# Norm's factor on GpSimd with a power, and a search that compares key less base with a constant table

## The chip, the cores and the metric

The kernel runs on one core of a Trainium2 chip. The metric is the device time of one execution in microseconds. Names of the engines in the rows: PE is TensorE, PEld its weight loads, DVE is VectorE, ACT is ScalarE, POOL is GpSimd, SP issues plain DMAs.

## What is computed

Three blocks on 3072 tokens of 512 features:

```python
# 1: attention in chunks of 32, with 16 left, 8 right and 8 memory keys
a = np.exp(scores - max);  a = a / (a.sum(-1) + 1e-9);  x = a @ v_full
# 2: routing: (token, expert) pairs by falling logit, 8 experts, at most 384 tokens each
for idx in np.argsort(-(x @ w_gate).flatten()):
    tok, e = idx // E, idx % E
    if assigned[tok] >= 0 or counts[e] >= cap: continue
    assigned[tok] = e; counts[e] += 1
out[assigned == e] = np.maximum(x[assigned == e] @ w1[e], 0) @ w2[e]
# 3: on that result
h = out @ w_in;  solu = h * softmax(h)
ln = (solu - mu) / np.sqrt(var + 1e-6) * g_ln;  y = ln @ w_out
```

## The kernel before

*Attention* (to about 146 us) works on 128 tokens at a time and ends with the gate's logits L in SBUF. *Route* then fills one expert a round: each token goes by its best expert left, as a 32-bit key, and `search` finds the largest 16-bit number that 384 keys of some expert reach, four bits at a time, first in the keys' upper half and then in the lower. There are 8 steps (it 0 to 3, twice) for each of seven experts; the eighth takes what is left.

One step: ge compares 24 keys of each partition with 15 thresholds (thr, or the constant table jtab in step 0); matrix products r count them by expert. For the first two experts there are 24 products and a second one ("sat", "some"). For the other five (`few`) there are 3 products, then on DVE d (the products' diagonal), n (its sum), q (n spread for the next product), one product, cmax and mx, the number of thresholds reached. From mx come the next thr, with jb (table plus base, made while PE counts), and the new base, lines 605 to 664.

*Experts*, in the order in which they fill: gather 384 tokens, `g12` (products h and y with w1 and w2), `g3` (w_in) with `soft` (c and the sums), `g4` (w_out) and a scatter of the rows ob. All products use a split of each operand into a high and a low part: ACT copies w1h and w2h, POOL subtracts (w1l, w2l, 128x512 each, 16 an expert), DVE makes hl, ll, xl and yl. POOL's queue also issues the indirect DMAs: weights, tokens, and the scatters behind a small memset (spacer). `norm`, line 1044, makes the factor k of each token from the sums in ss and sq, with 18 DVE instructions (na, nv, ny, nz, k; an inverse root by a shift and three Newton steps): once for three tiles together (3 columns), for the last expert once for each tile. k is read by the ACT instruction that makes ob, at the end of `g4` one stage later.

The order is not written out: `Pace` keeps a rough clock of each engine (its cost of each instruction is in `cost`, line 308) and emits the steps of routing, soft, norm and weight splits between PE's products when their inputs should be there. Each engine then runs in that order, so a product r that comes before its DVE input is ready holds up PE. Stage r, in what follows, is the stretch with g12 of expert r: stage 0 from 196 to 270 us, 1 to 335, and from there each runs from the start of one g4 to the next, 2 to 404, 3 to 482, 4 to 562, 5 to 642, 6 to 720. In stage r DVE also carries the search for expert r + 1 and, from stage 1 on, the norm of expert r - 1; in stages 0 and 1 the chunks of w_out too (v, e, out_l).

Of the kernel before, what the change touches and what calls it, by code (L numbers as in the profile page):

```python
# [10 lines left out]
F32 = mybir.dt.float32  # L11
# [18 lines left out]
DFF = 1024  # L30
# [25 lines left out]
def warm(nc, p, ident, n):  # L56
    """Keeps the tensor engine busy while it waits, so that its clock is up when the data come."""
    for i in range(n):
        nc.tensor.transpose(p[:, i % 4], ident, ident)


def attention(nc, tc, q, kx, vx, wgx, ident, x_dram, L, consts, beside):
    """Chunked attention of all heads, 128 tokens at a time, x to DRAM and the gate's logits to L."""
# [182 lines left out]
class Pace:  # L246
    """Work emitted in small steps beside the main products, when what it reads is about to be there.

    Each engine executes in program order, so that an instruction emitted too early holds up all that follows
    on its engine. A rough model of the core says when: the clocks (us) are where each engine will be after  # L250
    what has been emitted, "now" is the tensor engine's. A job is a generator. It yields what its next step
    waits for: a tile, an engine (the end of its last instruction), a time, or ("spare", engine): that the
    engine has nothing else to do."""
# [10 lines left out]
    def tile(self, ap):  # L264
        """Start, writes and reads of a tile. It starts when the tile before it in its place is done with."""
        t = self.tiles.get(ap.name)
        if t is None:
            start = 0.0
            if ap.space != DRAM:
                ring = self.rings.setdefault(ap.tensor.tag, [])  # L270
                bufs = ap.tensor.tag_meta.bufs
                if len(ring) >= bufs:
                    old = self.tiles[ring[-bufs]]
                    start = max([old[0]] + [x[4] for x in old[1] + old[2]]) + SIGNAL
                ring.append(ap.name)
            t = self.tiles[ap.name] = (start, [], [])
        return t
# [10 lines left out]
    def when(self, ap, eng="pe", write=False):  # L288
        """When ap can be read (or written) by the engine."""
        start, writes, reads = self.tile(ap)  # L290
        p0, p1, f0, f1 = self.region(ap)
        for w in writes + reads if write else writes:
            if w[0] < p1 and p0 < w[1] and w[2] < f1 and f0 < w[3]:
                start = max(start, w[4] + (SIGNAL if w[5] != eng else 0.125 if eng != "pe" and not write else 0.0))
        return start
# [88 lines left out]
    def soon(self):  # L384
        """When work that goes before will be there, less what a step may take."""
        return min([1e9] + [j[0] for j in self.jobs if j[2] < 2 and j[0] > self.now]) - self.fit

    def ready(self, *aps):
        """Lets time pass until the tensor engine finds these written."""
        while max(self.when(x) for x in aps) > self.now:  # L390
            self.tick()


class Timed:
    """The engines of nc, each instruction charged to pace."""
# [22 lines left out]
class Fixed:  # L418
    """w_in, and w_out times the norm's gain, each as a float32r part and the rest as another.

    The host hands over the float64 as they are: sign, 11 bits of exponent and the high 20 of the mantissa,
    then the low 32. Read as a float32 and times 2^-112 the first word has the exponent in its place but for
    three bits (v, once shifted); the second times the power of two is what v lacks."""
# [20 lines left out]
    def all(self, m, beside, every, a, b, lead=0.0):  # L444
        """Starts a chunk every so many us."""
# [68 lines left out]
    def need(self, m, beside, chunks):  # L514
        """Waits for these chunks, ahead of other work."""
# [5 lines left out]
    def take(self, what, n):  # L521
        """A place for one tile more, once one of n is free."""
# [5 lines left out]
class Route:  # L528
    """Greedy assignment by logit with a cap per expert, one expert filled per round.

    Each token left goes by its best expert left. The largest logit is sought (as a 32-bit key, four bits
    at a time, the keys' upper half and then the lower) above which some expert has CAP such tokens:
    that expert takes them, and what is left is the same problem."""
# [53 lines left out]
    def take(self):  # L587
        """The bank, when no other count is in it."""
# [8 lines left out]
    def search(self, key, oh, zero, r, late):  # L597
        """The largest 16-bit number that CAP keys of some expert reach; flags of such experts go on.

        few: of eight token tiles at once the products, then their sum by expert and threshold to all partitions,  # L600
        for fewer passes of the tensor engine; otherwise the way with the shortest chain."""
# [3 lines left out]
        base, thr, few, mid = zero, self.jtab[:, 0], late > LATE, NT if r else NT // 2  # L605
        for it in range(4):
            ge = self.t("ge", [NT, 15], BF)
            for c in (0,) if r else (0, mid):
                V.tensor_tensor(ge[:, c:c + mid], key[:, c:c + mid, None].to_broadcast([128, mid, 15]),
                                thr[:, None, :].to_broadcast([128, mid, 15]), op=ALU.is_ge)  # L610
            if last:
                last()
            if it < 3:
                jb = self.t("jb", [15])
                V.tensor_scalar(jb, self.jtab[:, it + 1], base, None, op0=ALU.add)
            yield "dve"
            p = yield from self.take()
            if few:
                for c in range(0, NT, 8):
# [5 lines left out]
                                op=ALU.mult)  # L625
                self.held = False
                n = self.t("n", [E], F16)
                with nc.allow_low_precision(reason="whole numbers up to 384"):
                    V.tensor_reduce(n[0:120], d[0:120].rearrange("p c e -> p e c"), axis=AX.X, op=ALU.add)
                q = self.t("q", [15, E], F16)  # L630
                V.tensor_tensor(q[0:120], n[0:120, None, :].to_broadcast([120, 15, E]), self.diag[0:120], op=ALU.mult)
# [26 lines left out]
            if it < 3:  # L658
                thr = self.t("thr", [15])
                V.scalar_tensor_tensor(thr, mx.to_broadcast([128, 15]), float(16 ** (3 - it)), jb,  # L660
                                       op0=ALU.mult, op1=ALU.add)
            nb = self.w.tile([128, 1], F32, tag="base", name="base", bufs=2)
            V.scalar_tensor_tensor(nb, mx, float(16 ** (3 - it)), base, op0=ALU.mult, op1=ALU.add)
# [113 lines left out]
    def compact(self, r, s1, sl):  # L777
        """The tokens taken, s1, by their slots sl: slot t * 128 + p to idx[p, t]."""
# [42 lines left out]
class Experts:  # L821
    """MoE of the experts in the order in which they fill, and the second block on their tokens."""

    def __init__(self, ctx, nc, tc, x_dram, w1, w2, fixed, route, beside, ident, out):
# [20 lines left out]
        self.spacer = k.tile([1, 1], F32, name="spacer")  # L845
        self.idx, self.iw = route.idx, route.iw
# [39 lines left out]
    def fetch(self, r, weights=True):  # L886
        """The tokens and the first weights of an expert, once they are known."""
# [22 lines left out]
    def bank(self, spare=False):  # L910
        """The transposes' bank, once its last tile is read; or one that is spare at the start."""
# [88 lines left out]
    def soft(self, r, t, h):  # L1000
        """c = h * exp(h - max) less its mean over the features; the sums that norm() takes.

        By halves, the maximum of the first while the products of the second run."""
# [34 lines left out]
        if r == E - 1:  # L1038
            yield 2.5
# [4 lines left out]
    def norm(self, r, s):  # L1044
        """k = 1/(sum+1e-9) / sqrt(var+1e-6), the token's factor of its output."""
        nc = self.nc
        ss, sq, k = (x[:, s] for x in self.Kc[r])
        s0, s1 = ss[:, :, 0], ss[:, :, 1]
        a, v, y, z = (self.sm.tile([128, TT], F32, tag=n, name=n, bufs=3)[:, s] for n in ("na", "nv", "ny", "nz"))
        V = nc.vector  # L1050
        V.scalar_tensor_tensor(a, s0, 1e-9, s1, op0=ALU.add, op1=ALU.add)
        yield 0.0
        V.reciprocal(a, a)
        yield 0.0
        V.tensor_tensor(v, a, a, op=ALU.mult)
        yield 0.0
        V.scalar_tensor_tensor(v, sq, 1.0 / DFF, v, op0=ALU.mult, op1=ALU.mult)
        yield 0.0
        V.tensor_scalar(v, v, 1e-6, None, op0=ALU.add)
        yield 0.0  # L1060
        V.tensor_scalar(y.bitcast(I32), v.bitcast(I32), 1, None, op0=ALU.logical_shift_right)
        V.tensor_scalar(v, v, -0.5, None, op0=ALU.mult)
        yield 0.0
        V.tensor_scalar(y.bitcast(I32), y.bitcast(I32), -1, 0x5F3759DF, op0=ALU.mult, op1=ALU.add)
        for _ in range(3):
            yield 0.0
            V.tensor_tensor(z, y, y, op=ALU.mult)
            yield 0.0
            V.tensor_tensor(z, z, v, op=ALU.mult)
            yield 0.0  # L1070
            V.scalar_tensor_tensor(y, z, 1.5, y, op0=ALU.add, op1=ALU.mult)
        yield 0.0
        V.tensor_tensor(k, a, y, op=ALU.mult)
# [44 lines left out]
    def run(self, steps):  # L1118
        """steps: the routing, a piece at a time, beside the products."""
# [110 lines left out]
def host(q, k, v, mem_k, mem_v, moe_w_gate, moe_w1, moe_w2, moe2_w_in, moe2_w_out, moe2_g_ln):  # L1230
    """Layouts of the inputs, in the types that they come in."""
# [45 lines left out]
```

## Time and profile before

| | |
|---|---|
| median of 3 runs | 859.87 us (857.61 to 862.3) |
| span of the profiled execution | 854.8 us |
| PE busy | 739.8 us, 87% |
| DVE busy | 563.6 us, 66%, 1667 instructions |
| POOL busy | 355.7 us, 42%, 360 instructions |
| chain that ended last | PE 55%, DVE 28%, DMA 10% |

A single time of the profiled execution is not listed beside the runs; its span is the time from its first instruction to its last, 5.1 us less than the median. All rows have line 406, since one helper records each operation: they are told apart by the tiles' names. An instruction's time counts from when its engine took it up to its end, so a wait inside it, for a port say, is part of it; a wait for a semaphore stands in brackets as idle time.

### The profile page before, as it was taken

To read this page: it belongs to the slowest core of one execution; us is meant where nothing else is said; L and a number is where in the kernel's file an instruction comes from. 1 tells how busy PE (TensorE), PEld (TensorE's weight loads), DVE (VectorE), ACT (ScalarE), POOL (GpSimd) and SP (SyncE) were. 2 spreads that over 40 slices of the span, in tenths; PEclk is the share of its full clock that TensorE was granted. 3 is DMA by queue.
4 is the path that set the end of the run, shared out by engine and by line. 5 is a ranking of instruction groups with operands and counts; after the bars stand their busy time and mean duration, and the time that the engine had idled before them with its cause. 6 is when DMAs were issued, how large, how long until landed. Compare 5 with 4: busy or idle time off the path is not lost.

```text
span 854.8 us, 14882 instructions
## 1 busy us (share of the span) xinstructions
PE 739.8 (87%) x5729; PEld 631.0 (74%) x5729; DVE 563.6 (66%) x1667; ACT 346.3 (41%) x681; POOL 355.7 (42%) x360
## 2 busy tenths in 40 slices
PE   5676787368998889899998999899899989999994
PEld 4555565257786777688887888788788889899883
DVE  6446466967999998789179838864984673163071
ACT  1344454122346444433183236324532643274170
POOL 6123232375556432652464146425532653464100
PEclk7899799557999999999999999999999999999997
DMA  9999899252135101510340042014101411330000
GB/s 204 238 240 224 200 218 362 90 181 87 38 114 173 35 13 38 184 50 1 105 166 2 14 156 103 1 58 165 50 1 62 162 48 38 115 120 1 38 1 37
DMA packets 37894, 88.32 MB, mean 103 GB/s; under 512 B 3904, under 2 KB 16320, under 8 KB 37824
## 3 DMA queue, kind: packets, MB, share of 16 engines
q1 hardware_dynamic: 24768, 41.23, 19.0%
q0 software_dynamic: 13056, 46.14, 16.2%
q8 instruction: 45, 0.74, 0.4%
q14 instruction: 25, 0.20, 0.1%
HBM read 74.78 MB, written 12.58 MB: 102 GB/s over the span
## 4 chain that ended last, share of the span: by engine, by line
PE 55%; DVE 28%; DMA 10%; issue 3%; SPq 1%; POOL 0%; ACT 0%; POOLq 0%; DVEq 0%
PE h L406 22%; PE o L406 16%; PE y L406 9%; DMA vd<-in_vx_dram 8%; DVE e L406 4%; PE r L406 3%; DVE ge L406 2%; PE tp L406 2%; DVE nz L406 2%; DVE q L406 2%; DVE thr L406 1%; DVE cmax L406 1%; DVE ohl L406 1%; DMA raw<-in_win_dram 1%; DVE hl L406 1%
## 5 line engine op out<-in xcount | busy, mean ns | idle before, releaser
L406 POOL TENSOR_TENSOR w1l<-raw,w1h 128x512 fp32r<-128x512 f32 x64 | 85.8, 1341 | 106.4 <-ACT w1h L406 103.9
L406 POOL TENSOR_TENSOR w2l<-raw,w2h 128x512 fp32r<-128x512 f32 x64 | 83.8, 1310 | 63.0 <-ACT w2h L406 60.7
L406 PE MATMUL y<-hh,w2h 128*128 128x384 f32 x256 | 92.0, 359 | 0.2 <-DVE e L406 0.2
L406 PE MATMUL y<-hl,w2h 128*128 128x384 f32 x256 | 89.8, 351 | 1.2 <-DVE hl L406 1.2
L406 PE MATMUL y<-hh,w2l 128*128 128x384 f32 x256 | 88.5, 346 | 0.0
L406 DVE TENSOR_REDUCE nm<-h 128x1 f32<-128x512 f32 x48 | 33.0, 687 | 77.0 <-PE h L406 77.0
L406 POOL DMA_INDIRECT out_dram<-ob,idx x24 | 24.5, 1022 | 136.6 <-ACT ob L406 135.5
L406 PE MATMUL o<-out_h,lh 128*128 128x512 f32 x192 | 77.0, 401 | 0.0
L406 PE MATMUL h<-in_h,yh 128*128 128x512 f32 x192 | 77.0, 401 | 0.0
L406 PE MATMUL h<-in_l,yh 128*128 128x512 f32 x192 | 76.1, 396 | 0.0
L406 PE MATMUL h<-in_h,yl 128*128 128x512 f32 x192 | 75.9, 395 | 0.0
L406 PE MATMUL o<-out_l,lh 128*128 128x512 f32 x192 | 75.1, 391 | 0.0
L406 PE MATMUL o<-out_h,ll 128*128 128x512 f32 x192 | 75.0, 391 | 0.0
L406 ACT ACTIVATE hh<-h 128x384 fp32r<-128x384 f32 x64 | 31.4, 491 | 101.7 <-PE h L406 91.1
L406 POOL DMA_INDIRECT raw<-in_w_dram,iw x64 | 62.8, 982 | 23.1 <-issue 15.7
L406 ACT CAST w2h<-raw 128x512 fp32r<-128x512 f32 x64 | 39.4, 618 | 64.7 <-PE y L406 38.8
L406 PE MATMUL h<-xh,w1l 128*128 128x384 f32 x256 | 64.0, 363 | 0.0
L406 PE MATMUL h<-xh,w1h 128*128 128x384 f32 x256 | 60.1, 355 | 0.7 <-ACT xh L406 0.7
L406 PE MATMUL h<-xl,w1h 128*128 128x384 f32 x256 | 60.5, 354 | 0.0
L406 POOL TENSOR_TENSOR p<-p,rec 128x512 f32<-128x512 f32 x22 | 22.9, 1042 | 79.8 <-DVE rec L406 56.3
L406 DVE SCALAR_TENSOR_TENSOR hl<-h,hh 128x384 fp32r<-128x384 f32 x64 | 35.2, 550 | 27.9 <-ACT hh L406 27.9
L406 PEld LDWEIGHTS y<-hl,w2h 128*128 128x128 f32 x256 | 49.1, 192 | 1.7 <-DVE hl L406 1.5
(197 smaller groups left out, 1771.2 us busy)
## 6 DMA issues: line engine op xcount, KB each, us to landing
vd<-in_vx_dram SPq DMA_DIRECT2D x48, 256.0 KB, 10.0
x_dram<-xs SPq DMA_DIRECT2D x6, 1024.0 KB, 9.0
kd<-in_kx_dram SPq DMA_DIRECT2D x12, 464.0 KB, 10.3
qt<-in_q_dram SPq DMA_DIRECT2D x6, 768.0 KB, 13.9
raw<-in_win_dram SPq DMA_DIRECT2D x16, 256.0 KB, 9.7
raw<-in_wout_dram SPq DMA_DIRECT2D x16, 256.0 KB, 2.7
qt<-in_q_dram SPq DMA_DIRECT2D x6, 256.0 KB, 6.8
kd<-in_kx_dram SPq DMA_DIRECT2D x8, 144.0 KB, 6.3
```

Of the source, the lines that this page charges most:

```text
L406: return fn(*args, **kw)
```

## The change

`norm` becomes six POOL instructions in place of 18 on DVE; the last is a power with exponent -0.5 from a constant tile, which one memset on DVE fills. The last expert's delay of 2.5 us ahead of it goes. In `search`, ge compares key less base with the table row of its step, so that thr and jb go; base is made by another form of instruction; n is written into the bank of the counts (PSUM, f32) and q reads it there. The comments of the functions are emptied too, which shifts line numbers.

```diff
@@ search
-        base, thr, few, mid = zero, self.jtab[:, 0], late > LATE, NT if r else NT // 2
+        base, few, mid = zero, late > LATE, NT if r else NT // 2
-                V.tensor_tensor(ge[:, c:c + mid], key[:, c:c + mid, None].to_broadcast([128, mid, 15]),
-                                thr[:, None, :].to_broadcast([128, mid, 15]), op=ALU.is_ge)
+                V.scalar_tensor_tensor(ge[:, c:c + mid], key[:, c:c + mid, None].to_broadcast([128, mid, 15]), base,
+                                       self.jtab[:, it, None, :].to_broadcast([128, mid, 15]),
+                                       op0=ALU.subtract, op1=ALU.is_ge)
-            if it < 3:
-                jb = self.t("jb", [15])
-                V.tensor_scalar(jb, self.jtab[:, it + 1], base, None, op0=ALU.add)
+                n = p[0:120, 8 * E:9 * E]
+                V.tensor_reduce(n, d[0:120].rearrange("p c e -> p e c"), axis=AX.X, op=ALU.add)
+                q = self.t("q", [15, E], F16)
+                V.tensor_tensor(q[0:120], n[:, None, :].to_broadcast([120, 15, E]), self.diag[0:120], op=ALU.mult)
                 self.held = False
-                n = self.t("n", [E], F16)
-                with nc.allow_low_precision(reason="whole numbers up to 384"):
-                    V.tensor_reduce(n[0:120], d[0:120].rearrange("p c e -> p e c"), axis=AX.X, op=ALU.add)
-                q = self.t("q", [15, E], F16)
-                V.tensor_tensor(q[0:120], n[0:120, None, :].to_broadcast([120, 15, E]), self.diag[0:120], op=ALU.mult)
-            if it < 3:
-                thr = self.t("thr", [15])
-                V.scalar_tensor_tensor(thr, mx.to_broadcast([128, 15]), float(16 ** (3 - it)), jb,
-                                       op0=ALU.mult, op1=ALU.add)
-            V.scalar_tensor_tensor(nb, mx, float(16 ** (3 - it)), base, op0=ALU.mult, op1=ALU.add)
+            V.tensor_scalar(nb, mx, float(16 ** (3 - it)), base, op0=ALU.mult, op1=ALU.add)
@@ Experts.__init__
+        self.power = k.tile([128, TT], F32, name="power")
+        nc.vector.memset(self.power, -0.5)
@@ soft
         if r == E - 1:
-            yield 2.5
             yield from self.norm(r, slice(t, t + 1))
@@ norm (all 18 instructions of before go; a yield stands between each of these)
+        G.tensor_tensor(a, ss[:, :, 0], ss[:, :, 1], op=ALU.add)
+        G.tensor_scalar(a, a, 1e-9, float(np.sqrt(1e-6 * DFF)), op0=ALU.add, op1=ALU.mult)
+        G.tensor_tensor(v, a, a, op=ALU.mult)
+        G.tensor_tensor(v, v, sq, op=ALU.add)
+        G.tensor_scalar(v, v, 1.0 / DFF, None, op0=ALU.mult)
+        G.tensor_tensor(k, v, self.power[:, s], op=ALU.pow)
```

DVE before, in stage 3 (about 447 to 451 us): the end of a search's second step, its third ge, the start of the norm, and the third step's q.

```order
L406 TENSOR_REDUCE cmax_6551<-r_6548 128x15
L406 TENSOR_SCALAR cmax_6551,mx_6553<-cmax_6551 128x15
L406 SCALAR_TENSOR_TENSOR thr_6555<-mx_6553,jb_6484 128x15
L406 SCALAR_TENSOR_TENSOR base_6557<-mx_6553,base_6480 128x1
L406 TENSOR_TENSOR ge_6559<-ki_6418,thr_6555 128x360
L406 TENSOR_SCALAR jb_6561<-jtab_150,base_6557 128x15
L406 SCALAR_TENSOR_TENSOR na_6580<-s_6294 128x3
L406 RECIPROCAL na_6580<-na_6580 128x3
L406 SCALAR_TENSOR_TENSOR hl_6571<-h_6537,hh_6570 128x384
L406 TENSOR_TENSOR d_6595<-r_6587,own_157 120x64
L406 TENSOR_REDUCE n_6597<-d_6595 120x8
L406 TENSOR_TENSOR q_6599<-n_6597,diag_166 120x120
```

DVE in the changed kernel, the same place: the second step's cmax to the third step's q.

```order
L406 TENSOR_REDUCE cmax_6358<-r_6353 128x15
L406 TENSOR_SCALAR cmax_6358,mx_6360<-cmax_6358 128x15
L406 TENSOR_SCALAR base_6362<-mx_6360,base_6291 128x1
L406 SCALAR_TENSOR_TENSOR ge_6364<-ki_6234,base_6362,jtab_150 128x360
L406 SCALAR_TENSOR_TENSOR hl_6375<-h_6345,hh_6374 128x384
L406 TENSOR_TENSOR d_6397<-r_6389,own_157 120x64
L406 TENSOR_REDUCE r_6389<-d_6397 120x8
L406 TENSOR_TENSOR q_6400<-r_6389,diag_166 120x120
```

thr, jb and the two na are gone; base has moved from behind thr to where thr stood, and ge follows it.

POOL before, in the same stage (about 443 to 453 us): two loads of weights and the subtractions of the next expert.

```order
L406 DMA raw1_5574<-in_w1_dram,iw3_5073 128x1024
L406 DMA raw2_5576<-in_w2_dram,iw3_5073 128x1024
L406 TENSOR_TENSOR w1l_5589<-raw1_5351,w1h_5588 128x512
L406 TENSOR_TENSOR w2l_5620<-raw2_5353,w2h_5619 128x512
L406 TENSOR_TENSOR w1l_5666<-raw1_5355,w1h_5665 128x512
L406 TENSOR_TENSOR w2l_5720<-raw2_5353,w2h_5719 128x512
```

POOL in the changed kernel, the same place (na, nv and k are the norm's, power the constant).

```order
L406 DMA raw1_5429<-in_w1_dram,iw3_4935 128x1024
L406 DMA raw2_5431<-in_w2_dram,iw3_4935 128x1024
L406 TENSOR_TENSOR w1l_5444<-raw1_5213,w1h_5443 128x512
L406 TENSOR_TENSOR w2l_5474<-raw2_5215,w2h_5473 128x512
L406 TENSOR_TENSOR na_5510<-s_5236 128x3
L406 TENSOR_SCALAR na_5510<-na_5510 128x3
L406 TENSOR_TENSOR nv_5511<-na_5510 128x3
L406 TENSOR_TENSOR nv_5511<-nv_5511,q_5237 128x3
L406 TENSOR_SCALAR nv_5511<-nv_5511 128x3
L406 TENSOR_TENSOR k_5238<-nv_5511,power_2018 128x3
L406 TENSOR_TENSOR w1l_5514<-raw1_5217,w1h_5513 128x512
L406 TENSOR_TENSOR w2l_5557<-raw2_5215,w2h_5556 128x512
```

The six instructions of the norm stand between a w2l and a w1l; the order of the rest is as before.

## Rows read from the trace of the kernel before

**Rows 1.** Page, part 1: busy us of each engine (share of the span) xinstructions.

```profile
PE 739.8 (87%) x5729; PEld 631.0 (74%) x5729; DVE 563.6 (66%) x1667; ACT 346.3 (41%) x681; POOL 355.7 (42%) x360
```

**Rows 2.** Busy us by stage: stretch, length, engines' busy (x), PEclk, DMA share, GB/s.

```profile
146.00:180.00 34.00, 12.39 (x249) 11.19 (x250) 30.32 (x127) 4.71 (x13) 15.76 (x16) 0.54 0.47 156
196.00:270.00 74.00, 66.53 (x493) 56.53 (x493) 65.61 (x171) 32.22 (x67) 41.19 (x40) 0.91 0.33 107
270.00:335.40 65.40, 58.25 (x336) 50.10 (x337) 60.79 (x193) 30.57 (x64) 22.03 (x20) 0.97 0.08 25
335.40:403.70 68.30, 61.41 (x363) 54.03 (x362) 55.77 (x166) 27.82 (x52) 34.26 (x33) 0.98 0.26 85
403.70:482.15 78.45, 75.01 (x407) 64.72 (x406) 51.52 (x172) 32.68 (x63) 35.03 (x34) 1.00 0.23 75
641.78:720.40 78.62, 75.43 (x428) 67.06 (x427) 44.94 (x117) 33.23 (x65) 38.70 (x36) 0.98 0.26 82
```

**Rows 3.** Waits of PE, 403.7 to 482.15 us: us in total, times, longest.

```profile
PE r L406 <- DVE q L406: 2.3, 4, 1.0
PE r L406 <- DVE ge L406: 0.9, 2, 0.7
```

**Rows 4.** Timeline, PE, DVE and POOL by turns: start, us, engine, operation, [idle before <-releaser].

```profile
349.24 5.61 DVE L406 TENSOR_TENSOR nz<-ny 128x3 f32<-128x3 f32 x1
...
349.83 1.29 POOL L406 TENSOR_TENSOR w1l<-raw,w1h 128x512 fp32r<-128x512 f32 x1
...
357.06 0.51 PE L406 MATMUL r<-oh,ge 128*120 128x64 bf16 x3 [3.40 <-DVE ge L406]
```

**Rows 5.** Timeline of stage 3 around one q and one thr.

```profile
449.78 1.28 POOL L406 TENSOR_TENSOR w1l<-raw,w1h 128x512 fp32r<-128x512 f32 x1 [1.85 <-ACT w1h L406]
...
449.85 1.28 DVE L406 TENSOR_TENSOR q<-n,diag 120x120 f16<-120x120 f16 x1
...
451.19 0.23 PE L406 MATMUL r<-q,ones 120*128 120x120 f16 x1 [0.58 <-DVE q L406]
...
452.36 0.86 PE L406 MATMUL h<-xh,w1l 128*128 128x384 f32 x4
...
454.74 0.17 DVE L406 SCALAR_TENSOR_TENSOR thr<-mx,jb 128x15 f32<-128x15 f32 x1
...
454.95 0.53 DVE L406 TENSOR_TENSOR ge<-ki,thr 128x360 bf16<-128x360 uint16 x1
```

**Rows 6.** Instructions by tile, DVE: xcount, duration ns min/median/max, first and last start.

```profile
L406 DVE TENSOR_TENSOR nz<-ny x30: 152/161/5609, 285.3 to 836.2; 128x3 f32<-128x3 f32 x21, 128x1 f32<-128x1 f32 x9
...
L406 DVE SCALAR_TENSOR_TENSOR thr<-mx,jb x30: 173/388/1070, 274.6 to 632.1; 128x15 f32<-128x15 f32 x30
...
L406 DVE TENSOR_TENSOR q<-n,diag x40: 220/222/1784, 272.3 to 634.3; 120x120 f16<-120x120 f16 x40
...
L406 DVE TENSOR_SCALAR jb<-jtab,base x28: 222/226/1256, 150.9 to 629.3; 128x15 f32<-128x15 f32 x28
...
L406 DVE TENSOR_TENSOR ge<-ki,thr x24: 332/532/880, 149.7 to 614.5; 128x360 bf16<-128x360 uint16 x18, 128x180 bf16<-128x180 uint16 x6
...
L406 DVE TENSOR_TENSOR d<-r,own x40: 208/213/226, 271.7 to 633.8; 120x64 f16<-120x64 f32 x40
...
L406 DVE SCALAR_TENSOR_TENSOR v<-v,e x32: 374/416/1512, 59.5 to 318.3; 128x256 int32<-128x256 int32 x32
```

**Rows 7.** The same for POOL, one tile.

```profile
L406 POOL TENSOR_TENSOR v<-v,in_h x16: 722/731/1513, 63.2 to 192.2; 128x256 f32<-128x256 f32 x16
```

**Rows 8.** Timeline, POOL: a DMA issue that waited for POOL's own w1l.

```profile
681.85 0.97 POOL L406 DMA_INDIRECT raw<-in_w_dram,iw  x1 [0.16 <-POOL w1l L406]
```

**Rows 9.** Timeline of the end: the last k and its reader.

```profile
836.75 0.16 DVE L406 TENSOR_TENSOR k<-na,ny 128x1 f32<-128x1 f32 x1
...
842.86 0.69 ACT L406 ACTIVATE ob<-o,k 128x512 f32<-128x512 f32 x1 [4.80 <-PE o L406]
```

More of the change, by code (lines that the diff above doesn't have):

```diff
@@ L1044, in norm @@
     def norm(self, r, s):
-        nc = self.nc
+        G = self.nc.gpsimd
         ss, sq, k = (x[:, s] for x in self.Kc[r])
[L1048 to L1051, printed above, removed]
+        a, v = (self.sm.tile([128, TT], F32, tag=n, name=n, bufs=3)[:, s] for n in ("na", "nv"))
+        G.tensor_tensor(a, ss[:, :, 0], ss[:, :, 1], op=ALU.add)
         yield 0.0
-        V.reciprocal(a, a)
+        G.tensor_scalar(a, a, 1e-9, float(np.sqrt(1e-6 * DFF)), op0=ALU.add, op1=ALU.mult)
         yield 0.0
-        V.tensor_tensor(v, a, a, op=ALU.mult)
+        G.tensor_tensor(v, a, a, op=ALU.mult)
         yield 0.0
-        V.scalar_tensor_tensor(v, sq, 1.0 / DFF, v, op0=ALU.mult, op1=ALU.mult)
+        G.tensor_tensor(v, v, sq, op=ALU.add)
         yield 0.0
-        V.tensor_scalar(v, v, 1e-6, None, op0=ALU.add)
+        G.tensor_scalar(v, v, 1.0 / DFF, None, op0=ALU.mult)
         yield 0.0
[L1061 to L1073, printed above, removed]
+        G.tensor_tensor(k, v, self.power[:, s], op=ALU.pow)
         for t in range(s.start, s.stop):
```

## The prediction

> **What bounds the kernel now.** I read the page's first part, then the busy times by stage, then the waits of PE in a stage, and last the timeline of DVE and GpSimd (POOL in the rows) around those waits. The page puts PE at 87% and DVE at 66% of 854.8 us [rows 1]. The stages say where that share hides a bound [rows 2]. From 146 to 180 us PE works 12.4 of 34.0 us: the first expert is sought and DVE's chain is the bound. From 196 us on PE sets the pace and only its gaps can be won: 74.00 - 66.53 = 7.5 us in stage 0, 65.40 - 58.25 = 7.2 in stage 1, 68.30 - 61.41 = 6.9 in stage 2, and 3.4 in stage 3 (78.45 - 75.01). Two more stages are like stage 3, and stage 6 has 3.2. That makes 13.5 us in stages 3 to 6 and 35 us from 196 to 720 us. The gaps of stage 3 are waits of the counting products r for DVE: 2.3 us for q and 0.9 us for ge [rows 3]. After 720 us no count is left.
>
> Why DVE is late there is the reading on which the rest stands. In stage 2 one nz, on 3 columns, takes 5.61 us, while POOL goes through its subtractions one after another from 349.83 us on; PE then stands 3.40 us in front of the first r [rows 4]. In stage 3 a q takes 1.28 us, as long as the w1l that POOL started just before it, and PE stands 0.58 us [rows 5]. Over the whole run nz has 0.152 us at best and 5.609 at worst, q 0.220 and 1.784, thr 0.173 and 1.070; d, as wide as a half of q but with one of its two inputs in PSUM, has 0.208 and 0.226 in 40 cases [rows 6]. So a DVE instruction that reads two tensors in SBUF waits out a POOL instruction, and one with an input in PSUM does not.
>
> **The norm.** 18 DVE instructions go, for seven experts on 3 columns and three times on 1. At nz's median of 0.161 us [rows 6] one norm is 18 x 0.161 = 2.9 us of DVE, and its waits come on top. In stage 3 its parts stand between the counts (the first order block of the change). They go for good.
>
> On POOL six instructions come, in one piece between two subtractions. Nothing of so few columns that reads tensors is in the trace there, and no power. A subtraction of 512 columns takes 1.28 us [rows 5] and one of 256 at best 0.722 [rows 7]: 2.2 ns a column, which leaves 0.16 us for the instruction itself. Each of the six waits for the one before; where POOL waited for its own result the gap was 0.16 us [rows 8]. I take 0.33 us each, 2.0 us a norm. The bounds: 1.0 us with no gaps; 6 x (0.72 + 0.16) = 5.3 us if each costs as much as 256 columns, the nearest full row; for the power alone I know no better end. Behind them in the queue stand w1l, w2l and then the DMAs of the next weights. What hides them: POOL sat idle 1.85 us before w1l at 449.78 us, and PE takes a w1l at 452.36, 1.3 us after that one's end [rows 5]: 3.15 us of room, or about 2.2 when PE gets there 1 us sooner (its waits at q gone). So 2.0 us fits closely, and I charge 1 us in all for seven norms.
>
> On that six the Trainium skill (GPSIMD Engine Reference, section 2.1 Instruction dispatch) adds one warning: the first call of newly loaded code on these cores costs about 6 us, unseen in the profile. No run here shows it; an estimate from that figure is one late w1l, some 4 us once, and a time near 848 us.
>
> The last expert's norms are off the path: k is ready at 836.75 us and its reader ob starts at 842.86 [rows 9], 6 us later. POOL's order puts a scatter of 0.97 us inside the last norm; that still fits. No gain and no loss there.
>
> **The search.** 42 thr and 42 jb go (14 searches, 3 each). What this is worth on the chain is little: ge starts 0.21 us after thr (454.74 to 454.95 [rows 5]), and now it has to follow base in the same way, so the chain keeps its length. thr's wait for POOL does not vanish: its median in the trace is 0.388 us against 0.173 at best, and ge, which still reads key and table from SBUF, inherits those 0.2 us. The jb, 0.226 us each, stood behind ge while PE counted; they delayed hl and e only. ge itself changes its form. The nearest row of the new form with two SBUF inputs is v, 256 columns in 0.416 us; ge's 360 in 0.532 us lie on the same line (104 columns more for 0.116 us) [rows 6], so I charge nothing; the bound above is its worst case so far, 0.880.
>
> A sentence of the skill speaks against that: in the Vector Engine (DVE) Microarchitecture Reference, section 7, this form with two SBUF sources that are not bf16 runs at half rate. The row of v says otherwise, since 256 columns at half of DVE's rate would be some 0.53 us without any start-up. I follow the row and keep the rule as a rival.
>
> n is now written to PSUM, and q reads it there. n I leave at 0.27 us. q loses its fast form: by d's 0.213 us for 64 columns and 1.1 ns for each of 56 more it takes 0.27 us in place of 0.222, and it no longer waits for POOL. Over 40 cases that is +2 us of DVE against waits of up to 1.78 us. The ge waits remain.
>
> **The sum**, in PE's gaps. Stages 3 to 6: of 13.5 us I leave 1.25 a stage (the ge waits as they are, and a rest), so -8.5. Stage 2: the 3.40 us behind nz, and 0.6 of the rest, -4.0: m and ge of that search now run before POOL's series begins. Stage 1: DVE is 60.79 us busy in 65.4, and loses a norm (2.9 us and waits) and 8 x (0.23 + 0.17) = 3.2 us; I take half of the gap, -3.5. Stage 0: its search reads counts from PSUM and its thr never waited; -0.5. The first search, 146 to 180 us: the same chain, 0 (from -1, if ge meets POOL less often, to +1.5, if more often). POOL +1. Together -15.5 us: the profiled execution would go from 854.8 to 839.3. The median of the runs, 859.87, lies 5.1 us above that span, so 844.4 us. The ends: all gaps from 196 us on gone gives 825; every term nothing and POOL's upper bound gives more than before.
>
> **The rivals.**
> First, the waits move: ge takes what thr and q waited, and PE waits for ge. For it: 40 ge with two SBUF inputs stay in the same places beside the same subtractions. Against: q's four waits a stage are the larger half, and a q cannot wait any more. Price: 40 x 0.2 = 8 us back, time 852. By the skill (SBUF — State Buffer, Who interferes with whom) two SBUF inputs contend with a POOL instruction that reads SBUF; the new norm is 60 such instructions more, which points this way.
>
> Second, slower: the norm on POOL. From 3.15 us a norm on, w1l comes late and PE waits at h in each of seven stages. At the bound of 5.3 us it is 3.1 us with PE's gain (5.3 - 2.2), 7 x 3.1 = 22 us, against which the gains of 16.5 stand: 865. Between, at 0.5 us an instruction, 3.0 a norm, it costs 6 us and the time is 849. For it: nothing shows a power on POOL. Against: the room in [rows 5].
>
> Third, ge at half rate, by the rule above: 360 columns at 1.1 ns more each make 0.39 us on 40 ge, and half of that on each of the 16 steps of the first two experts, some 19 us of chain, perhaps half of it before PE: 854.
>
> Fourth, more than I take: DVE gets ahead in stages 0 and 1 too, and the granted clock, 0.91 of full in stage 0 [rows 2], rises with fewer gaps: 10 us more, 834.
>
> **How the numbers follow.** My forecast 0.62, the moved waits 0.17, POOL slower 0.09, ge at half rate 0.04, the larger gain 0.08. Below 836 and above 857 I leave about a tenth each, so 836 to 857. What can be told from no change here is 0.5%, 4.3 us. Faster by more: the forecast, the larger gain and two thirds of the moved waits, 0.82; same 0.09, slower 0.09.
>
> **What would show it.** PE's gaps in stages 3 to 6 at 1 to 1.5 us each; no r behind a q; the 3.40 us before the first r of stage 2 gone; q never above 0.35 us; ge's mean up from 0.53 to 0.7 or so; six POOL instructions in about 2 us, and no h that waits for w1l. I am wrong if PE waits for w1l after each norm, if ge takes 0.9 us with POOL idle, or if the gaps stay and only their releaser changes from q to ge.

## The result, and the profile after

The changed kernel is faster, by more than was forecast. The first comparison, of four runs of each kernel, gave a ratio of 0.9691 [0.9648, 0.9733] to the kernel before; a second, six runs against 29 of before, gave 0.9782 [0.9742, 0.9822]. On 859.87 us these are 833 and 841 us, against a forecast of 844.4 and a range from 836: the first lies below the range, the second in it, and only 3 us from the forecast.

The two differ mainly in the kernel before, with a median of 861.1 us in the first and 854.7 in the second (839.2 and 836.4 for the changed kernel); why it was slower in the first is not shown. Slow runs are left out of the ratios, of the changed kernel's first four and of psum_only's the profiled one (844.97 and 860.08 us). In the profiles a part that the change does not touch varies: from the start to the first count of the search, the attention, the 14 profiled executions of this study take between 140.0 and 157.6 us. So the executions are compared from the first count to the end, and by stages; the changed kernel's second execution (span 833.4 us, attention 149.4) is shown, as its attention is nearest to that of before (148.2).

The page's first part, changed kernel (answers to [rows 1]):

```profile
PE 734.6 (88%) x5729; PEld 628.8 (75%) x5729; DVE 502.9 (60%) x1404; ACT 344.1 (41%) x681; POOL 376.3 (45%) x420
```

Busy times by stretch, in the columns of [rows 2]. Stages 0 and 1 are cut here at the expert's first product h, the later ones where a g4 starts. First the kernel before: from the first count to the end, stages 0 to 2 one by one, stages 3 to 6 in one piece.

```profile
148.22:854.80 706.58, 635.24 (x3783) 550.70 (x3783) 480.56 (x1462) 283.66 (x559) 307.07 (x296) 0.95 0.23 75
187.72:264.53 76.81, 70.80 (x504) 60.80 (x504) 68.35 (x171) 34.13 (x72) 46.13 (x44) 0.88 0.33 106
264.53:335.20 70.67, 60.30 (x349) 51.83 (x347) 66.02 (x203) 31.82 (x65) 24.59 (x23) 0.98 0.10 32
335.20:402.59 67.39, 60.50 (x348) 53.41 (x347) 54.83 (x166) 27.18 (x51) 34.26 (x33) 0.97 0.26 86
402.59:720.17 317.58, 304.11 (x1708) 263.51 (x1708) 211.41 (x655) 132.43 (x258) 144.22 (x136) 0.99 0.23 76
```

The changed kernel: first count to end, first search, stages 0 to 6 one by one, stages 3 to 6 in one piece.

```profile
149.43:833.43 684.00, 627.97 (x3783) 546.74 (x3783) 420.15 (x1198) 281.70 (x559) 328.04 (x356) 0.95 0.23 76
149.43:189.54 40.11, 16.92 (x271) 14.58 (x272) 30.26 (x111) 6.11 (x15) 20.35 (x20) 0.54 0.40 119
189.54:266.98 77.44, 69.92 (x503) 59.46 (x504) 65.18 (x163) 33.28 (x73) 45.36 (x44) 0.89 0.34 107
266.98:332.22 65.24, 58.92 (x352) 51.16 (x351) 61.09 (x179) 32.02 (x67) 32.23 (x34) 1.00 0.15 44
332.22:396.29 64.07, 59.66 (x344) 53.06 (x343) 43.74 (x126) 26.16 (x50) 32.17 (x35) 0.97 0.23 79
396.29:471.56 75.27, 75.00 (x420) 65.42 (x420) 46.67 (x148) 33.09 (x65) 37.34 (x40) 1.00 0.23 78
471.56:547.47 75.91, 75.60 (x432) 65.66 (x432) 49.53 (x153) 32.99 (x65) 37.40 (x39) 1.00 0.24 77
547.47:623.49 76.02, 75.60 (x433) 65.66 (x433) 49.51 (x154) 33.02 (x65) 37.47 (x39) 1.00 0.23 77
623.49:698.75 75.26, 73.79 (x428) 65.32 (x427) 38.33 (x93) 33.08 (x66) 41.43 (x42) 1.00 0.26 86
396.29:698.75 302.46, 299.98 (x1709) 262.05 (x1708) 184.04 (x547) 132.18 (x258) 153.65 (x160) 1.00 0.24 79
```

From the first count to the end 706.6 us have become 684.0: 22.6 us less (the other execution has 687.2, 19.4 less). Of these, 317.58 - 302.46 = 15.1 us lie in stages 3 to 6, where PE's gaps (length less PE's busy time) fell from 13.5 to 2.5 us. In stages 3 to 5 they are 0.3 to 0.4 us each, and PE there waits for no q and no ge [rows 3].

DVE by tile (answers to [rows 6]: min/median/max in ns):

```profile
L406 DVE SCALAR_TENSOR_TENSOR ge<-ki,base,jtab x24: 393/689/3575, 151.0 to 596.6; 128x360 bf16<-128x360 uint16 x18, 128x180 bf16<-128x180 uint16 x6
L406 DVE SCALAR_TENSOR_TENSOR ge<-lo,base,jtab x24: 401/594/1582, 160.7 to 611.9; 128x360 bf16<-128x360 f32 x18, 128x180 bf16<-128x180 f32 x6
...
L406 DVE TENSOR_TENSOR q<-r,diag x40: 281/283/284, 273.6 to 613.6; 120x120 f16<-120x120 f32 x40
L406 DVE TENSOR_SCALAR base<-mx,base x30: 212/214/216, 280.1 to 615.3; 128x1 f32<-128x1 f32 x30
...
L406 DVE TENSOR_SCALAR lo<-ki,base x7: 229/629/1231, 158.3 to 600.5; 128x24 f32<-128x24 uint16 x7
```

ge still waits, as forecast. q never does, and neither does base, whose waits the prediction had not looked at; lo, which reads one tensor and base by a pointer, does. POOL's norm and a ge ahead of it, in the stage that [rows 5] shows of before:

```profile
440.00 1.29 POOL L406 TENSOR_TENSOR w2l<-raw,w2h 128x512 fp32r<-128x512 f32 x1
...
440.54 1.14 DVE L406 SCALAR_TENSOR_TENSOR ge<-ki,base,jtab 128x360 bf16<-128x360 uint16 x1
441.25 0.48 POOL L406 TENSOR_TENSOR na<-s 128x3 f32<-128x3 f32 x1
...
441.82 0.20 POOL L406 TENSOR_SCALAR na<-na 128x3 f32<-128x3 f32 x1
442.10 0.19 POOL L406 TENSOR_TENSOR nv<-na 128x3 f32<-128x3 f32 x1
442.37 0.20 POOL L406 TENSOR_TENSOR nv<-nv,q 128x3 f32<-128x3 f32 x1
442.65 0.24 POOL L406 TENSOR_SCALAR nv<-nv 128x3 f32<-128x3 f32 x1
442.98 0.90 POOL L406 TENSOR_TENSOR k<-nv,power 128x3 f32<-128x3 f32 x1
443.86 1.28 POOL L406 TENSOR_TENSOR w1l<-raw,w1h 128x512 fp32r<-128x512 f32 x1
```

The norm takes 443.86 - 441.25 = 2.6 us, and no h waits for a w1l. At the end, k is ready 3 us before its reader (6 before, [rows 9]), so the tail of both is the same:

```profile
812.34 0.57 POOL L406 TENSOR_TENSOR k<-nv,power 128x1 f32<-128x1 f32 x1
815.97 0.69 ACT L406 ACTIVATE ob<-o,k 128x512 f32<-128x512 f32 x1 [3.60 <-PE o L406]
```

### The profile page after: what moved, and what is told of

It is laid out like the page before. It is cut to its first block, busy times and chain, and to the rows that moved or that the text cites. A ratio compares the mean times of both kernels' runs of the same rounds, so it can differ in the third digit from the quotient of the medians.

```text
span 843.0 us, 14682 instructions
## 1 busy us (share of the span) xinstructions
PE 735.2 (87%) x5729; PEld 630.4 (75%) x5729; DVE 502.6 (60%) x1404; ACT 343.9 (41%) x681; POOL 375.7 (45%) x420
## 3 DMA queue, kind: packets, MB, share of 16 engines
q1 hardware_dynamic: 24768, 41.23, 19.3%
## 4 chain that ended last, share of the span: by engine, by line
PE 59%; DVE 21%; DMA 13%; issue 3%; ACT 2%; SPq 1%; POOL 1%; POOLq 0%; DVEq 0%; ACTq 0%
PE h L406 25%; PE o L406 15%; PE y L406 11%; DMA vd<-in_vx_dram 5%; DVE e L406 3%; DVE ge L406 3%; PE tp L406 3%; PE r L406 3%; DMA kd<-in_kx_dram 2%; DVE ohl L406 2%; DMA raw<-in_win_dram 2%; DMA qt<-in_q_dram 1%; DVE hl L406 1%; DMA xg<-x_dram,idx 1%; PE s L406 1%
## 5 line engine op out<-in xcount | busy, mean ns | idle before, releaser
L406 POOL TENSOR_TENSOR w2l<-raw,w2h 128x512 fp32r<-128x512 f32 x64 | 86.4, 1350 | 47.6 <-ACT w2h L406 46.4
L406 PE MATMUL h<-xh,w1l 128*128 128x384 f32 x256 | 61.1, 357 | 0.0
L406 PE MATMUL r<-oh,ge 128*15 128x8 bf16 (+1 forms) x504 | 25.8, 180 | 30.5 <-DVE ge L406 30.0
```

Of the source, the lines that this page charges most:

```text
L406: return fn(*args, **kw)
```

## The experiments

Theory A, the prediction's: a DVE instruction that reads two tensors in SBUF waits out a POOL instruction, and PE's gaps are those waits. Rival B: DVE is simply loaded, and any 3 us less would do. A third cause stood beside both: the order, that is which DVE instruction meets which subtraction.

All runs in one table, in us. "First count to end" leaves the attention out. "DVE's waits" are the mean of stages 3 to 5: for each DVE instruction its time less the shortest of the same tile and shape, summed where it is over 0.06 us. The last four columns stand on one execution of each kernel. The changed kernel's other execution has 687.2, 302.6, 2.5 and 2.4, so the stages repeat better than the third column; the ratios do not all follow that column either (norm_only is 4.8 us shorter than before in it, and 0.55% slower over twelve runs), and a few us in it show nothing.

| kernel | ratio to before | first count to end | stages 3-6 | PE's gaps there | DVE's waits a stage |
|---|---|---|---|---|---|
| before | | 706.6 | 317.6 | 13.5 | 8.3 |
| changed | 0.9782 [0.9742, 0.9822] | 684.0 | 302.5 | 2.5 | 2.4 |
| norm_only | 1.0055 [1.0028, 1.0082] | 701.8 | 317.2 | 14.3 | 8.8 |
| search_only | 0.9931 [0.9902, 0.9961] | 698.5 | 315.1 | 13.4 | 5.6 |
| psum_only | 0.9975 [0.9948, 1.0002] | 700.4 | 314.6 | 13.2 | 7.1 |
| ge_only | 1.0100 [1.0058, 1.0142] | 709.2 | 323.9 | 19.3 | 8.1 |
| dve_free18 | 0.9835 [0.9797, 0.9874] | 684.3 | 308.7 | 6.9 | 3.6 |
| dve_port18 | 1.0028 [0.9992, 1.0064] | 703.7 | 316.2 | 14.3 | 6.5 |
| after_oldbase | 0.9822 [0.9781, 0.9863] | 689.3 | 310.4 | 9.9 | 5.6 |
| before_halves | 0.9944 [0.9910, 0.9979] | 697.7 | 318.4 | 12.0 | 7.4 |
| before, norm 4 us later | 0.9910 [0.9879, 0.9941] | 696.5 | 310.2 | 9.2 | 6.7 |
| changed, norm 4 us later | 0.9729 [0.9655, 0.9803] | 680.7 | 302.7 | 3.4 | 2.6 |
| table_in_psum | 0.9694 [0.9648, 0.9740] | 674.2 | 300.8 | 2.1 | 1.5 |

**The changed kernel again.** No edit.

> The changed kernel once more, for a second profile and more runs. Theory A (PE's gaps in stages 3 to 6 are what it gains; in the first profile a stage there is 76.0 us long with 0.4 us of gaps, against 79.8 and 3.4 before): the four stages again come to some 302 us against 316.8, and from the first count of the search to the end the kernel takes 687 us against 706.6, so about 20 us are won after the attention and nothing in it (148 us of attention as before): ratio 0.975 to 0.979. Rival B (the change also shortens something ahead of the stages): the attention or the first search is shorter than the 148.2 and 39.5 us of before by 5 us or more, ratio 0.970 or less.

684.0 us from the first count and 302.5 in the four stages: theory A's numbers. Neither the attention (149.4) nor the first search (40.1) is shorter than before.

**The parts alone.** norm_only takes the new norm, search_only the new search, psum_only and ge_only the two halves of the search (code shortened here and below):

```
psum_only:  n = p[0:120, 8 * E:9 * E]            # n and q as in the change; thr, jb, base, norm as before
ge_only:    V.scalar_tensor_tensor(ge, key, base, jtab, op0=subtract, op1=is_ge)   # thr, jb gone, new base;
                                                                                    # n, q, norm as before
```

> Only the norm goes to GpSimd; the search is the one of before. Theory A (the gaps are waits of q, thr and nz behind GpSimd; the norm brings the 3.4 us of stage 2, the search brings stages 3 to 6): PE's gaps in stages 3 to 6 keep 2 us or more of their 3.4, since q and thr still read two tensors in SBUF; 5 to 8 us are won, ratio 0.991 to 0.994. Rival B (DVE's load: any 3 us less per stage would do, since DVE then is ahead of PE): the gaps of stages 3 to 6 fall below 1 us with the norm alone, 15 us or more are won, ratio 0.982 or less. Rival C (the norm costs on GpSimd): h waits for w1l, ratio 1.0 or more.

> Only the search changes (comparison of key less base, count in PSUM); the norm stays on DVE. Theory A: q no longer waits for GpSimd, thr and jb are gone; gaps of stages 3 to 6 fall from 3.4 to 1 us or so each, stage 2 keeps the 3.4 us behind nz; 8 to 12 us won, ratio 0.986 to 0.991. Rival B (DVE's load): 3 us less per stage as well (9 us of busy time over the run for jb and thr each some 15), so the gaps fall by about half, 6 us won, ratio 0.993. If norm alone and search alone add up to the whole (20 us), the parts act by themselves; if each alone brings most of it, what counts is that DVE is early enough once.

> Only n is written to PSUM and q reads it there; thr, jb, ge and the norm are as before. Theory A: the 2.3 us a stage that PE waits at q go in stages 3 to 6 (q at most 0.3 us), the 0.9 us at ge stay: gaps 1.2 us a stage, 9 us won, ratio 0.989. Rival B (DVE's load): q is 0.06 us longer and the load is no smaller, so the wait goes to the next instruction and the gaps stay at 3 us: ratio 1.000.

> Only the comparison of key less base (thr and jb gone, base by a scalar); n and q in SBUF, norm on DVE as before. Theory A: q and nz still wait, base and thr no longer: stalls of stages 3 to 5 from 8.3 to 6 us, gaps of stages 3 to 6 of 10 to 13 us, 313 to 317 us. Rival B (thr and jb, or base, are the gain by themselves): 306 us or less.

In stages 3 to 6 the norm alone brings 0.3 us, the search alone 2.5, both 15.1; the comparison alone costs 6. Theory A missed the ratio of all four, and the gaps of all but norm_only. Rival B had psum_only right (gaps of 3.3 us a stage, 0.9975) and the ratio of search_only (0.9931), where the gaps did not fall as it said. The third cause named for norm_only, a late w1l, had its ratio (1.0 or more), but no h waits for w1l there. Neither A nor B had a part that makes the kernel slower. PE's waits in the four stages (us in total, times, longest), kernel before:

```profile
PE r L406 <- DVE q L406: 6.9, 12, 1.0
PE r L406 <- DVE ohl L406: 2.9, 3, 1.7
PE r L406 <- DVE ge L406: 2.8, 6, 0.7
```

search_only:

```profile
PE r L406 <- DVE ge L406: 7.5, 6, 1.9
PE r L406 <- DVE ohl L406: 3.0, 3, 1.7
PE r L406 <- DVE c L406: 2.3, 3, 0.8
```

and psum_only:

```profile
PE r L406 <- DVE ge L406: 8.2, 9, 2.0
PE r L406 <- DVE ohl L406: 2.9, 3, 1.7
PE r L406 <- DVE q L406: 1.3, 3, 0.5
```

The waits for q went to ge: the prediction's first rival came true in both, and not in the whole. One place in search_only shows how:

```profile
437.18 1.29 POOL L406 TENSOR_TENSOR w2l<-raw,w2h 128x512 fp32r<-128x512 f32 x1 [0.81 <-ACT w2h L406]
437.29 1.20 DVE L406 TENSOR_SCALAR ny<-nv 128x3 int32<-128x3 int32 x1
...
439.47 0.27 DVE L406 TENSOR_REDUCE cmax<-r 128x15 f32<-128x120 f32 x1
...
439.82 1.26 POOL L406 TENSOR_TENSOR w1l<-raw,w1h 128x512 fp32r<-128x512 f32 x1 [1.35 <-ACT w1h L406]
...
440.24 1.23 DVE L406 SCALAR_TENSOR_TENSOR ge<-ki,base,jtab 128x360 bf16<-128x360 uint16 x1
441.53 0.35 PE L406 MATMUL r<-oh,ge 128*120 128x64 bf16 x3 [1.93 <-DVE ge L406]
```

The norm's ny, which reads one tensor only, waits out w2l, cmax comes 1 us late for that, and so ge meets the next subtraction. In norm_only base does the same; its shortest is 0.146 us:

```profile
L406 DVE SCALAR_TENSOR_TENSOR base<-mx,base x30: 146/154/1301, 287.0 to 640.1; 128x1 f32<-128x1 f32 x30
```

**Load or port.** The changed kernel with eighteen DVE instructions that do no work of the kernel in each norm of experts 0 to 6, of two kinds:

```
dve_free18:  V.tensor_scalar(dz, dz, 0.5, ss[:, 0, 0:1], op0=mult, op1=add)    # dz: 1 column
dve_port18:  V.tensor_tensor(dz, dz, ss[:, :, 0], op=min)                      # dz: 3 columns
```

> The changed kernel, and with each norm of experts 0 to 6 eighteen more DVE instructions of one column whose second operand is a pointer to a scalar (the form of the new base, which took 0.212 to 0.216 us in all 30 cases and so never waited): 3.9 us of DVE a norm, as many instructions as the old norm had. They do no work of the kernel. Theory A (ports: what costs is a DVE instruction that can wait for GpSimd, and load does not): DVE's stalls in stages 3 to 5 stay near 2.5 us, PE's gaps below 1 us a stage, stages 3 to 6 together 303 to 305 us (302.5 in the changed kernel). Rival B (load and queue: eighteen instructions between the counts delay the next one, whatever they read): gaps of 3 us a stage again as with the search alone, 314 us or more.

> The same with eighteen DVE instructions of three columns that read two tensors in SBUF (the form of nz, 0.16 us): 2.9 us of DVE a norm, less load than in the run beside it. Theory A: they wait behind GpSimd as nz did, 3 to 4 us of stalls a stage more, and PE's gaps come back to 2 to 3.4 us a stage: 310 to 315 us in stages 3 to 6. Rival B (load): no more than in the run beside it; if both stay below 1 us a stage, it was the chance of the order and neither port nor load.

The first kind never waits, the second as nz did:

```profile
L406 DVE TENSOR_SCALAR dz<-dz,s x126: 200/214/216, 283.5 to 750.1; 128x1 f32<-128x1 f32 x126
```

```profile
L406 DVE TENSOR_TENSOR dz<-dz,s x126: 148/161/1273, 286.4 to 772.5; 128x3 f32<-128x3 f32 x126
```

In stages 3 to 6 the longer ones cost 6.2 us, the shorter ones 13.8. From the first count to the end the longer ones cost nothing that shows (684.3; the ratio's interval overlaps that of the changed kernel), the shorter ones 20 us (703.7). So load is refuted as the main cause. The two kinds differ in columns as well as in tensors; what the second tensor does by itself is shown by base, below. A missed dve_free18's stages 3 to 6 by 4 to 6 us, B by 5: 308.7 us, with these waits of PE:

```profile
PE r L406 <- DVE ge L406: 2.5, 6, 0.6
PE r L406 <- DVE c L406: 2.3, 3, 0.8
```

They stand in the round's second half, where counts now come a little later and their ge, and the oc from which c is made, meet a subtraction; dve_port18 has the same 2.3 us at c. We read that as load that acts through the order; no run holds the order fixed. In this execution the time from the first count to stage 3 was 6.2 us shorter than in the changed kernel's, which hides it in the whole.

**The instruction that was overlooked.** The changed kernel with base in its old form, two tensors in SBUF:

```
-V.tensor_scalar(nb, mx, float(16 ** (3 - it)), base, op0=mult, op1=add)
+V.scalar_tensor_tensor(nb, mx, float(16 ** (3 - it)), base, op0=mult, op1=add)
```

> The changed kernel with base made in its old form (two tensors in SBUF: mx and base) in place of a scalar by pointer. Theory A: a second instruction of each step stands open to GpSimd; base takes up to 1.3 us again, the stalls of stages 3 to 5 go from 2.4 to 4 or so and PE's gaps from 0.3 to 1 or 2 us a stage, stages 3 to 6 some 306 us. Rival B (only the norm's and q's waits count, base is too short to matter): the old form is 0.06 us shorter, gaps stay at 0.3, 302.5 us.

```profile
L406 DVE SCALAR_TENSOR_TENSOR base<-mx,base x30: 159/398/1219, 273.9 to 616.6; 128x1 f32<-128x1 f32 x30
```

One column, 0.06 us shorter at best, and it brings back 8.0 us in stages 3 to 6, 7.4 of them gaps. That is A, at more than the size it gave. Over the whole it does not show clearly: first count to end it is 5.3 us, since stage 2 is 4 us shorter there, and the ratio's interval overlaps that of the changed kernel.

**How long one wait is.** The kernel before with each subtraction in two of 256 columns:

```
+for c in (slice(0, 256), slice(256, 512)):
+    nc.gpsimd.tensor_tensor(lo[:, c], raw[:, c], h.bitcast(F32)[:, c], op=subtract)
```

> The kernel before with each subtraction w1l and w2l on GpSimd cut in two of 256 columns (same values). Theory A (a DVE instruction waits for the end of the GpSimd instruction that is running): no single wait is above 0.75 us where it was 1.1, unless GpSimd's next instruction goes first as in the 5.6 us case; stalls of stages 3 to 5 fall from 8.3 to 5 us, gaps from 3.4 to 2 a stage. Rival B (the DVE instruction waits until GpSimd pauses): waits as long as before or longer, gaps 3.4 or more.

In stages 3 to 5 no wait is above 0.61 us where 12 of 39 were above 0.75; but there are 53 now, 7.4 us a stage in place of 8.3. The size of a wait is A's; the gaps fell by 1.5 us, not by the 5.6 of a fall from 3.4 to 2 a stage, and the four stages are no shorter (318.4). More subtractions are met.

**How much is the order.** Both kernels with the norm emitted 4 us later (one line, `yield 4.0`, ahead of it):

> The kernel before with each norm of experts 0 to 6 emitted 4 us later. If the gaps of before (13.5 us in stages 3 to 6) were an unlucky order, they can be half of it: 310 us in place of 317.6. If the many instructions that can wait are the reason, 12 to 16 us of gaps stay, 316 to 320 us.

> The changed kernel with each norm of experts 0 to 6 emitted 4 us later. If the small gaps of stages 3 to 6 (2.5 us in all) were a lucky order, another order brings back several us: 306 to 312 us in place of 302.5. If few instructions that can wait are the reason, the four stages stay within 302 to 304 us.

Before, the four stages take 310.2 us, the number given ahead for an unlucky order: 7.4 us less, 4.3 of them gaps. After, another order moves them by 0.3 us and the gaps by 0.9. With one other order of each, the small gaps are no luck as far as this shows, but about half of the 15.1 us that the change gains there over before was the bad order of before.

**One step on.** In the changed kernel the counts get a fixed bank of PSUM, its last columns hold a copy of ge's table:

```
+self.jps = self.bank[:, 448:508].rearrange("p (i j) -> p i j", i=4);  V.tensor_copy(self.jps, self.jtab)
-self.jtab[:, it, None, :].to_broadcast([128, mid, 15])
+self.jps[:, it, None, :].to_broadcast([128, mid, 15])
```

> The changed kernel with ge's table read from a copy in PSUM (a fixed bank for the counts, its last columns hold the table), so that ge too has only one input in SBUF. Theory A (ports): no ge above 0.65 us any more where the worst was 3.58 us; PE's waits for ge go where they still stand: 2.6 us at the third ge of stage 2, 1.4 and 1.0 us in stage 1; from the first count to the end 684 us become 677 to 680, ratio to the kernel before 0.968 to 0.974. Rival B (DVE is late there for other reasons): the same 684 us, or more if a table in PSUM makes ge longer.

```profile
L406 DVE SCALAR_TENSOR_TENSOR ge<-ki,base,r x24: 393/589/592, 153.2 to 589.2; 128x360 bf16<-128x360 uint16 x18, 128x180 bf16<-128x180 uint16 x6
L406 DVE SCALAR_TENSOR_TENSOR ge<-lo,base,r x24: 396/590/592, 162.8 to 604.3; 128x360 bf16<-128x360 f32 x18, 128x180 bf16<-128x180 f32 x6
```

No ge waits. Against the changed kernel, first count to end, 9.8 us less: 3.2 of them in stage 0 and 4.4 in stage 2; but stage 2 is as short (59.9 us, against 59.7) in after_oldbase, so that part is not shown to be ge's. It is the fastest version here: 828.9 us against 836.4 of the changed kernel, with before at 854.4 and 854.7 beside them. Its ratio [0.9648, 0.9740] lies below that of the changed kernel in its larger comparison; the smaller one gave 0.9691.

## Why the prediction was right in direction and too small

**The step that failed** is the term of stages 3 to 6: "of 13.5 us I leave 1.25 a stage (the ge waits as they are, and a rest), so -8.5". It measured -15.1: 11.0 of gaps, 4.1 of PE's busy time (304.11 to 299.98). Two readings behind it were wrong, and two things were left out.

"And now it has to follow base in the same way, so the chain keeps its length" missed that base changes its form too, from two tensors to a pointer. With base put back (after_oldbase) 8.0 of the 15.1 us are gone; the 7.2 that stay are near the 8.5 of the forecast.

"The ge waits remain" held for DVE and not for PE. In the shown stage ge loses up to 0.54 us (0.97 us a stage) and PE loses none; with the norm 4 us later PE loses 1.8 us in all. Our reading: with one such instruction left in a step, its wait mostly ends before PE comes for it; with four (thr, base, ge, q) and a norm between, one wait makes the next, as ny, cmax and ge in the place shown of search_only. So the gain isn't a sum over instructions, as the prediction's was: the table's parts do not add up.

The gaps of before were taken as fixed, while 4.3 us of them were the order (before, norm 4 us later). And the 4.1 us of PE's busy time were in no term. 1.6 of it is stage 6, where the granted clock was 0.98 before and 1.00 after. The other 2.5 us, 0.8 to 1.0 a stage, come in psum_only and search_only as well, with the same instructions; why stays open.

The larger comparison's total (-18.6 us, 0.0218 of 854.7, against -15.5) is near the forecast by luck: the terms are not. Of the first one's 26.6 us, 4 to 7 lie in nothing behind the first count; what they are is not shown.

**The other terms.** Stage 2: -3.3 against -4.0. The 3.40 us behind nz are gone, but a ge there now has the run's longest wait:

```profile
356.04 0.95 POOL L406 DMA_INDIRECT raw<-in_w_dram,iw  x1 [0.31 <-issue]
...
356.32 3.58 DVE L406 SCALAR_TENSOR_TENSOR ge<-ki,base,jtab 128x360 bf16<-128x360 uint16 x1
356.99 1.29 POOL L406 TENSOR_TENSOR w1l<-raw,w1h 128x512 fp32r<-128x512 f32 x1
...
358.23 1.27 POOL L406 TENSOR_TENSOR w2l<-raw,w2h 128x512 fp32r<-128x512 f32 x1
...
359.95 0.42 PE L406 MATMUL r<-oh,ge 128*120 128x64 bf16 x3 [2.59 <-DVE ge L406]
```

This is the first rival's moved wait, in one place. Stage 1: -5.4 (other execution -1.3, at a granted clock of 0.93 in place of 1.00) against -3.5; the 8 x (0.23 + 0.17) us there should be 6 x, 2.4 us, three thr and three jb a search, but the half of the gap that was taken does not hang on it. Stage 0: +0.6 and -0.4 against -0.5. First search: +0.6 against 0. The norm on POOL: 2.6 us each, between the 2.0 taken and the 3.15 of room, and nothing lost against +1; the second rival's price was not paid. Of the late w1l priced at 4 us nothing is seen: the first norm takes 2.9 us (280.57 to 283.44), and its w1l follows at once. The tail: 134.6 and 134.7 us from the last cut to the end, as forecast.

**The third rival, ge at half rate.** ge took 0.594 us at its usual, against 0.532 in its old form: 0.06 more, not 0.39; with the table in PSUM it took 0.590. The Trainium skill (Vector Engine (DVE) Microarchitecture Reference, section 7) has this form at half rate; the trace disagrees.

**The mechanism** was right for two tensors in SBUF, and too narrow. The Trainium skill (SBUF — State Buffer, section Who interferes with whom) says that a DVE instruction with two SBUF inputs contends with a GpSimd instruction that reads SBUF, and one with at most one, outside the two-port modes, does not. dve_port18 beside dve_free18 agrees (1.273 and 0.216 us at most), and base, of one column in both forms, shows it with nothing else changed (1.219 and 0.216). What the prediction passed over stood in its own rows: jb reads one tensor and a pointer, and took up to 1.256 us [rows 6]. Others of that kind waited too, lo (1.231), es (0.73 in stage 3) and ny (1.20 in search_only), all on 3 columns or more; no run here shows in which mode they ran. Of one column none waited, base and dz in 30 and 126 cases.

## What to carry to other kernels

Where VectorE shares a stretch with a busy GpSimd, count the instructions on the chain that read two tensors in SBUF, also those of one column, and those of several columns that read one tensor and a scalar. Of these, the ones that never waited here had an operand in PSUM (d, q and ge with it there) or were of one column with a pointer (base); a pointer alone did not save jb and lo. Do it to all on the chain, since the wait of one left can take the place of those removed. An edit that adds up from single waits is not to be trusted while several such instructions follow each other: alone, the parts gained 3 us or less in stages 3 to 6, together 15. Before a gain is put down to such an edit, move something harmless: the norm 4 us later gave 7 of those 15 in the kernel before. When one part of a kernel varies by more than the effect, compare from behind that part.

## What the hardware showed that was not expected

- A waiting DVE instruction often gets its turn when the running GpSimd instruction ends, even where the next follows at once: in stage 3 ge went between w2l and na, and na took 0.48 us for it (0.20 in its median over the run). But not always: the ge of 3.58 us waited through a w1l and the w2l behind it, and nz [rows 4] through four subtractions. What decides it is not shown.
- The ge of 3.58 us was taken up 0.67 us ahead of w1l, beside an indirect DMA's issue. Such an issue does not by itself hold a ge up: others took 0.53 us beside one (kernel before, 195.54 us) and 0.59 (changed kernel, 197.38 us). Why this one did not finish first is not shown.
- On GpSimd the power on 3 columns takes 0.90 us, on one column 0.57; the other five instructions of the norm 0.19 to 0.24 in their medians.
- The time up to the first count varies by 17.7 us between the 14 executions, though all these kernels run the same attention.
